# Another list order for the first 1278 operations of a fused attention and feed-forward kernel

## The chip, the cores and the metric

The kernel runs on one core of a Trainium2 chip. The metric is the device time of one execution in microseconds (us). Five engines take part, each with its own in-order queue: TensorE (PE in the profile, its weight loads PEld), VectorE (DVE), ScalarE (ACT), GpSimd (POOL) and SyncE (SP). SP only issues transfers here; sixteen DMA engines carry them out.

## The reference

Two blocks follow each other, all in float32. The first is a lightning attention over 4 batches, 8 heads, 768 positions and a head width of 64; the second a feed-forward block with a leaky ReLU.

```python
for b in range(nb):                                  # blocks of 64 positions
    intra = einsum('bhic,bhjc->bhij', qb, kb) * Dmask
    intra = einsum('bhij,bhjd->bhid', intra, vb)
    inter = einsum('bhid,bhde->bhie', qb * lam_pow, kv_state)
    out[:, :, sl] = intra + inter
    kv_state = lam_block * kv_state + einsum('bhsd,bhse->bhde', kb * rev_pow, vb)
x = out.transpose(0, 2, 1, 3).reshape(3072, 512)
h = x @ w_in                                         # 512 -> 2048
return maximum(0.01 * h, h) @ w_out                  # 2048 -> 512
```

## The kernel before

The 3072 rows are cut into 24 chunks of 128 tokens (the code's `c`); four chunks make a group (`g`, six in all). For each chunk the kernel loads k, q and v (`load_kq` L464, `load_v` L524), transposes k and q on PE through PSUM (L546), copies them out (`kT`, `qT`; L527, on ACT or DVE), scales q by powers of the decay (`qsT`, L592), scales k (L585, on POOL or DVE), and then runs small 64 x 64 products, all recorded at line L410: the scores (`go`, into `psc`), the key-value products (`kv`, into two spare PSUM banks for the first four chunks), the chunk's own part of the output (`own`) and two halves of the part that comes from the state (`inter`, before and after a two-column read `seen_po`, L676). DVE masks the scores (L637) and adds to the states (L642, L644); POOL decays the states (L647). The attention output of a chunk is then split into three parts, `xh` (ACT, L692), `xl` (DVE, L700) and `xm` (DVE, L718).

A float32 product of the feed-forward block is three products of rounded parts: high, low and mixed. The weights `w_in` are cut into eight pieces (`wi` 0 to 7, 256 columns each). A piece is loaded in two halves of 512 KB into one of three `raw` buffers, turned from 64-bit to 32-bit floats by three ACT operations (L793, L795, L797) and two DVE operations (L799, L800) a half, and split into `wh` (L805, on ACT or DVE), `wm` and `wl` (L812, L814, on DVE). Function `up` (L850) multiplies the parts of a group by those of a piece: six blocks of four products for each pair of group and piece (for the very first pair, group 0 and piece 1, in two calls of half width, 256 columns). ACT applies the leaky ReLU (L877) and the result goes to DRAM (L880). When all is through, `down` (L916) reads it back, splits it and multiplies by the parts of `w_out`.

The order of all this is not written as loops. The functions only add operations to a list (`Plan.add`): engine or engines that may do it, a length, what it reads and writes. `Plan.emit` then makes the program. It first takes the entries of `ORDER` (L266), a list of pairs of an operation's number and its engine, in exactly that order; where an operation may run on two engines, the pair also says on which. What `ORDER` doesn't list is placed behind it by a greedy rule. Since every engine's queue is in order, `ORDER` sets the order within each queue, SP's included, which issues each transfer when its turn comes and its target is free. The PSUM banks and buffers that are not fixed are handed out in list order too. A negative entry is a filler: `(-n, "PE")` runs `busy(n, ...)` (L344 to L349), products of the identity with itself, n blocks of 64 columns wide, whose result nobody reads. A fixed filler of nine blocks (`busy(WARM, ...)`) opens the program.

The numbers used below: for chunk 0, loads of k, q, v are 3, 4, 5, the transposes 6 and 7, copies 8 and 9, scaled k 10, scaled q 11, scores 12, key-value products 13, masked scores 14, first state 15, own output 19, state part 20, `seen_po` 21, second state part 22. Chunk 1 has the same in 26 to 45, chunk 2 in 49 to 70, chunk 3 in 72 to 94. Operations 101 and 95 load the two halves of weight piece 1, 171 and 177 those of piece 0; 155 to 160 and 163 to 168 are the half-width blocks of the first `up`. Operation 163, the first such block on chunks 2 and 3, is used as a milestone.

Each filler and product is issued by one of these two lines (L349, L850):

```python
nc.tensor.matmul(wide[:, :k, :], lhsT=ident, rhs=_bc(ident[:, 0:C2], 1, k), start=True, stop=True, skip_group_check=True)
nc.tensor.matmul(dst, lhsT=w[z][:, kk * 2 * P + f * P:kk * 2 * P + (f + 1) * P], rhs=x[z][:, kk, toks], ...
```

Of the kernel before, what the change touches and what calls it, by code (L numbers as in the profile page):

```python
# [239 lines left out]
def kernel(  # L240
# [117 lines left out]
    plan = Plan(kinds, also, {"k@2": early[0], "v@2": early[0], "k@3": early[1], "v@3": early[1], "q@3": early[2]})  # L358
    plan.fill, plan.idle, plan.warm, plan.order = busy, None if ORDER else busy, 1.3 + 0.22 * WARM, ORDER
    add = plan.add  # L360
# [680 lines left out]
```

## Time and profile before

| | |
|---|---|
| time, three runs | 610.72 us median (610.02 to 610.86) |
| the profiled execution | 610.24 us, of which the span on the core is 608.5 us |
| mean granted PE clock | 0.997 |
| DVE, ACT, POOL busy over the span | 48%, 35%, 12% |
| DVE busy from 30 to 75 us | 40.55 of 45.00 us |
| DVE busy from 75 to 90 us | 6.37 of 15.00 us |

The profile's page gives the span, the busy time of each engine, and a chain: the work that ended last, followed backwards. Its timeline lists instructions in order with the idle time before them and what ended it, in brackets. A table by stretches gives, for each stretch of time, the busy time and number of instructions of each engine, the granted PE clock, the share of the DMA engines and the rate moved. Ends of PE instructions are modelled, so that consecutive ones overlap by some tenths of a microsecond; distances between starts are the safer measure.

### The profile page before, as it was taken

The numbers are of one execution on the slowest core, as the hardware profiler recorded it, in microseconds if no ns is written. First come the engines' busy times: TensorE is split into PE (matmuls) and PEld (weight loads), VectorE is DVE, ScalarE is ACT, GpSimd is POOL, SyncE is SP. The second block draws the span as 40 slices with busy tenths as digits, with TensorE's granted clock in tenths as the row PEclk, the third lists the DMA queues.
The fourth block names the chain that finished last, engine by engine and source line by source line (L and its number), as shares of the span: only waits on it lengthen the run. The fifth ranks groups of instructions, "written<-read, shape, count | busy, mean of one in ns | idle before, by whom it ended". The sixth has DMA issues, their size and how long they took to land.

```text
span 608.5 us, 12711 instructions
## 1 busy us (share of the span) xinstructions
PE 598.8 (98%) x5368; PEld 493.6 (81%) x5368; DVE 291.6 (48%) x405; ACT 210.0 (35%) x326; POOL 74.6 (12%) x86
## 2 busy tenths in 40 slices
PE   7899999999999999999999999999999999999997
PEld 5688888888888888888788888888888888888886
DVE  6898936243164333343366864344353443534530
ACT  4667752221433423443434422222222313214111
POOL 3332312204041132122000000000000000000000
PEclk9899999999999999999999999999999999999999
DMA  9999866676798878876297852524434343433201
GB/s 210 215 262 273 215 195 166 155 166 183 175 279 229 226 197 216 231 205 205 86 360 282 311 163 79 174 69 140 137 104 138 104 137 117 127 104 122 87 1 69
DMA packets 147753, 105.18 MB, mean 173 GB/s; under 512 B 123632, under 2 KB 124400, under 8 KB 147696
## 3 DMA queue, kind: packets, MB, share of 16 engines
q1 hardware_dynamic: 147408, 104.29, 58.9%
q8 instruction: 42, 0.69, 0.5%
q14 instruction: 15, 0.12, 0.1%
q10 hardware_dynamic: 288, 0.07, 0.0%
HBM read 68.69 MB, written 35.65 MB: 171 GB/s over the span
## 4 chain that ended last, share of the span: by engine, by line
PE 95%; DMA 2%; SPq 1%; DVE 1%; issue 0%; ACT 0%; DVEq 0%
PE b L850 33%; PE b L916 16%; PE psc L916 11%; PE po L916 11%; PE pt L850 10%; PE pt L916 5%; PE po L410 4%; PE psc L410 3%; DMA gs<-in_v_dram 1%; SPq L466 1%; DMA att<-in_v_dram 1%; PE po L546 0%; DVE w L800 0%; DVE xm L718 0%; PE b L546 0%
## 5 line engine op out<-in xcount | busy, mean ns | idle before, releaser
L898 DVE SCALAR_TENSOR_TENSOR xl<-att,xh 128x1024 fp32r<-128x1024 f32 x48 | 58.7, 1222 | 126.4 <-ACT xh L897 126.4
L897 ACT ACTIVATE xh<-att 128x1024 fp32r<-128x1024 f32 x48 | 50.7, 1061 | 147.6 <-PE pt L916 69.9
L850 PE MATMUL b<-xl,wl 128*128 128x512 f32 (+1 forms) x300 | 78.2, 387 | 0.0
L850 PE MATMUL b<-xh,wh 128*128 128x512 f32 (+1 forms) x300 | 77.3, 388 | 0.0
L850 PE MATMUL b<-xm,wm 128*128 128x512 f32 (+1 forms) x300 | 77.2, 386 | 0.0
L877 ACT ACTIVATE gs<-b 128x512 f32<-128x512 f32 x73 | 42.3, 596 | 88.2 <-PE b L850 57.8
L850 PEld LDWEIGHTS b<-xh,wh 128*128 128x128 f32 x300 | 54.8, 188 | 11.4
L850 PEld LDWEIGHTS b<-xl,wl 128*128 128x128 f32 x300 | 54.9, 188 | 11.2
L850 PEld LDWEIGHTS b<-xm,wm 128*128 128x128 f32 x300 | 54.9, 188 | 11.1
L900 DVE SCALAR_TENSOR_TENSOR xm<-xl,xh 128x1024 fp32r<-128x1024 f32 x48 | 58.8, 1226 | 4.8
L916 PE MATMUL b<-wh,xh 128*128 128x512 f32 x144 | 56.0, 389 | 0.0
L916 PE MATMUL b<-wl,xl 128*128 128x512 f32 x144 | 56.0, 389 | 0.0
L916 PE MATMUL b<-wm,xm 128*128 128x512 f32 x144 | 56.0, 389 | 0.0
L647 POOL TENSOR_TENSOR att<-att 128x256 f32<-128x256 f32 x40 | 28.7, 718 | 125.4 <-DVE att L644 105.2
L916 PE MATMUL psc<-wm,xm 128*128 128x512 f32 (+1 forms) x100 | 38.2, 387 | 0.0
L916 PE MATMUL po<-wm,xm 128*128 128x512 f32 (+1 forms) x100 | 37.9, 384 | 0.0
L916 PE MATMUL psc<-wh,xh 128*128 128x512 f32 x96 | 37.3, 389 | 0.0
L916 PE MATMUL psc<-wl,xl 128*128 128x512 f32 x96 | 37.3, 389 | 0.0
L916 PE MATMUL po<-wh,xh 128*128 128x512 f32 x96 | 37.3, 389 | 0.0
L916 PE MATMUL po<-wl,xl 128*128 128x512 f32 x96 | 37.3, 389 | 0.0
L410 PEld LDWEIGHTS po<-att 64*64 64x64 f32 x1408 | 26.5, 134 | 10.3 <-issue 7.0
L410 PE MATMUL po<-att 64*64 64x64 f32 x1408 | 32.2, 222 | 1.9 <-DVE att L676 1.3
(105 smaller groups left out, 858.8 us busy)
## 6 DMA issues: line engine op xcount, KB each, us to landing
att<-g SPq DMA_DIRECT2D x48, 512.0 KB, 3.5
g<-gs SPq DMA_DIRECT2D x47, 512.0 KB, 3.5
raw<-in_moe_w_in_dram SPq DMA_DIRECT2D x16, 512.0 KB, 5.6
raw<-in_moe_w_out_dram SPq DMA_DIRECT2D x16, 512.0 KB, 4.6
out_dram<-gs SPq DMA_DIRECT2D x23, 256.0 KB, 2.1
att<-in_k_dram SPq DMA_DIRECT2D x44, 128.0 KB, 4.2
att<-in_v_dram SPq DMA_DIRECT2D x22, 256.0 KB, 4.4
wo<-w SPq DMA_DIRECT2D x8, 512.0 KB, 5.9
```

The costliest lines, as they stand in the source:

```text
L410: nc.tensor.matmul(dst[HALF[cols]], lhsT=lhsT[HALF[rows]], rhs=rhs[HALF[rows]], start=start, stop=True, skip_group_check=True)
L466: nc.sync.dma_start(out=dst[:, z * HP:(z + 1) * HP, :], in_=y[z::2].rearrange("h p d -> p h d"))
L647: add("POOL", 0.62, lambda new=new, j=j: nc.gpsimd.tensor_tensor(state[(j + 1) % 4], new, _bc(lam_c, 2, D), op=ALU.mult), [f"st{j % 4}", " ...
L850: nc.tensor.matmul(dst, lhsT=w[z][:, kk * 2 * P + f * P:kk * 2 * P + (f + 1) * P], rhs=x[z][:, kk, toks], start=start and kk == 0, stop=kk ...
L877: add("ACT", ns, lambda b=b, r=r: nc.scalar.activation(out=r(), in_=b(), func=AF.Prelu, bias=0.0, scale=1.0, alpha=0.01), [kb], [kg], rank ...
L897: add("ACT", 1.05, lambda: nc.scalar.activation(out=h, in_=graw[j], func=AF.Copy, bias=0.0, scale=NEAR), reads, wr("h"))
L898: add("DVE", 1.215, lambda: nc.vector.scalar_tensor_tensor(l, graw[j], 1.0, h.bitcast(F32), op0=ALU.mult, op1=ALU.subtract), reads + [f"rh ...
L900: add("DVE", 1.215, lambda: nc.vector.scalar_tensor_tensor(m, l.bitcast(F32), -S, h.bitcast(F32), op0=ALU.mult, op1=ALU.add), [f"rh{j}", f ...
L916: nc.tensor.matmul(to[:, cols], lhsT=ring[j][z][:, f * T + tb * P:f * T + (tb + 1) * P], rhs=W[pp][z][:, f * d_model:(f + 1) * d_model][:, ...
```

## The change

Only `ORDER` is replaced. It lists 1278 operations in place of 1276 (1290 and 1291, two PE blocks of `up`, are new in it) and eight fillers in place of two: of 5, 4, 10, 4, 4, 5, 4 and 5 blocks, where there were 10 and 9. The work that is computed is the same.

Twelve operations change engine. From ACT to DVE go 9, 31, 32 (the copies of `qT` of chunk 0 and of `kT` and `qT` of chunk 1), 21 (`seen_po` of chunk 0), 141, 686 and 783 (later `seen_po`). From DVE to ACT go 272, 601, 922 (`seen_po`) and 324 and 399 (`wh` of pieces 4 and 6).

In SP's queue, the loads after the first half of weight piece 1 stood in the order v of chunk 1, k of chunk 2, second half of piece 1, q and v of chunk 2, q and k of chunk 3, first half of piece 0, q of chunk 4, second half of piece 0, v of chunk 3. They now stand: k and q of chunk 2, v of chunk 1, second half of piece 1, q of chunk 3, v of chunk 2, q of chunk 4, k and v of chunk 3, the two halves of piece 0.

On PE, the two transposes of chunk 0 change places, the scores of a chunk come earlier against the products of the chunk before it, and four half-width blocks of `up` (155 to 158) stand together ahead of the key-value products of chunk 3, where only one (155) did. The transpose of chunk 4's k (113) and its key-value products (128), which stood ahead of 163, come behind it; the scores of chunk 4 (129), which stood between 165 and 166, come behind 166. From some 300 blocks on the orders fall together again: the last 236 planned operations of PE, 105 of DVE, 79 of ACT and 81 transfers are the same.

```diff
-    ORDER = [(4, "DMA"), (0, "DVE"), (2, "DVE"), (3, "DMA"), (1, "DVE"), (26, "DMA"), (5, "DMA"), (-10, "PE"), (6, "PE"),
-      (27, "DMA"), (101, "DMA"), (7, "PE"), (29, "PE"), (8, "DVE"), (28, "DMA"), (9, "ACT"), (12, "PE"), (49, "DMA"), (31, "ACT"),
-      (10, "POOL"), (11, "DVE"), (13, "PE"), (30, "PE"), (33, "POOL"), (14, "DVE"), (15, "DVE"), (32, "ACT"), (19, "PE"), (20, "PE"),
-      (21, "ACT"), (35, "PE"), (34, "DVE"), (102, "ACT"), (95, "DMA"), (50, "DMA"), (51, "DMA"), (73, "DMA"), (16, "POOL"),
-      (72, "DMA"), (17, "DVE"), (105, "DVE"), (103, "ACT"), (22, "PE"), (37, "DVE"), (36, "PE"), (18, "POOL"), (23, "ACT"),
...
-      (82, "PE"), (64, "POOL"), (-9, "PE"), (81, "PE"),
...
+    ORDER = [(4, "DMA"), (3, "DMA"), (26, "DMA"), (0, "DVE"), (-5, "PE"), (7, "PE"), (1, "DVE"), (5, "DMA"), (2, "DVE"), (27, "DMA"),
+      (9, "DVE"), (-4, "PE"), (6, "PE"), (10, "POOL"), (101, "DMA"), (49, "DMA"), (8, "DVE"), (-10, "PE"), (12, "PE"), (11, "DVE"),
+      (14, "DVE"), (29, "PE"), (33, "POOL"), (13, "PE"), (31, "DVE"), (50, "DMA"), (15, "DVE"), (103, "ACT"), (19, "PE"), (102, "ACT"),
+      (30, "PE"), (28, "DMA"), (20, "PE"), (32, "DVE"), (95, "DMA"), (21, "DVE"), (34, "DVE"), (16, "POOL"), (73, "DMA"), (-4, "PE"),
+      (35, "PE"), (37, "DVE"), (22, "PE"), (52, "PE"), (-4, "PE"), (53, "PE"), (105, "DVE"), (104, "ACT"), (17, "DVE"), (23, "ACT"),
+      (106, "DVE"), (-5, "PE"), (36, "PE"), (54, "ACT"), (24, "DVE"), (55, "ACT"), (97, "ACT"), (58, "PE"), (18, "POOL"), (25, "DVE"),
+      (42, "PE"), (96, "ACT"), (38, "DVE"), (43, "PE"), (57, "DVE"), (98, "ACT"), (39, "POOL"), (44, "DVE"), (60, "DVE"), (45, "PE"),
+      (40, "DVE"), (46, "ACT"), (51, "DMA"), (111, "DMA"), (72, "DMA"), (56, "POOL"), (99, "DVE"), (100, "DVE"), (47, "DVE"), (76, "PE"),
+      (-4, "PE"), (59, "PE"), (41, "POOL"), (-5, "PE"), (114, "PE"), (74, "DMA"), (107, "ACT"), (48, "DVE"), (171, "DMA"), (65, "PE"),
+      (177, "DMA"), (61, "DVE"), (66, "PE"), (78, "ACT"), (116, "ACT"), (67, "ACT"), (108, "DVE"), (75, "PE"), (77, "ACT"), (68, "PE"),
+      (69, "ACT"), (109, "DVE"), (155, "PE"), (82, "PE"), (156, "PE"), (157, "PE"), (158, "PE"),
...
```

2 lines of the change are left out of this document (1 added, 1 removed).

## The prediction

> **What bounds the kernel now.** I read the page's head first, then who PE waits for, then a table by stretches, then PE's timeline.
>
> ```profile
> span 608.5 us, 12711 instructions
> PE 598.8 (98%) x5368; PEld 493.6 (81%) x5368; DVE 291.6 (48%) x405; ACT 210.0 (35%) x326; POOL 74.6 (12%) x86
> ...
> PE 95%; DMA 2%; SPq 1%; DVE 1%; issue 0%; ACT 0%; DVEq 0%
> ...
> PE po L410 <- DVE att L676: 1.3, 1, 1.3
> PE b L410 <- DMA att<-in_v_dram: 1.1, 1, 1.1
> PE b L410 <- DMA gs<-in_v_dram: 0.9, 1, 0.9
> ```
>
> PE is busy 598.8 of 608.5 us and makes up 95% of the chain, so only some 10 us are not PE work. The three longest of PE's waits but the one at the start are for a two-column read on DVE and for two loads of v (the last number of a row is the longest single wait). The table says where they lie:
>
> ```profile
> 11.50:19.70 8.20, 4.46 (x141) 3.64 (x140) 7.29 (x13) 6.61 (x11) 3.41 (x4) 0.98 0.93 212
> 19.70:23.10 3.40, 3.40 (x84) 2.64 (x84) 2.75 (x5) 1.38 (x3) 1.33 (x1) 0.55 1.01 244
> 23.10:28.50 5.40, 4.55 (x132) 3.46 (x127) 4.29 (x7) 4.17 (x8) 1.84 (x3) 1.00 0.98 239
> 28.50:34.30 5.80, 5.66 (x115) 4.79 (x107) 5.38 (x10) 3.30 (x7) 1.36 (x2) 1.00 1.04 297
> 34.30:75.00 40.70, 40.70 (x683) 34.30 (x676) 36.67 (x55) 28.98 (x53) 12.27 (x12) 1.00 0.91 246
> 75.00:304.70 229.70, 229.70 (x2759) 189.31 (x2758) 87.34 (x174) 82.14 (x147) 50.98 (x56) 1.00 0.72 194
> 304.70:608.50 303.80, 300.49 (x1329) 248.87 (x1327) 141.78 (x124) 79.98 (x98) 0.00 (x0) 1.00 0.42 141
> ```
>
> (Columns: stretch and length; busy time of PE, PEld, DVE, ACT, POOL; granted PE clock; DMA share; GB/s.) From 11.5 to 19.7 PE stands idle 3.74 of 8.20 us, then works 3.4 us at a clock of 0.55, then idles 0.85 more. From 34.3 to 304.7 it is never idle. DVE is nearly full too: 36.67 of 40.70 us up to 75 us; later it has room. So what can be won lies before 34 us, and what may take it away is DVE between 30 and 75 us.
>
> ```profile
> 12.60 0.69 PE L410 MATMUL b<-att 64*64 64x64 f32 x32 [1.09 <-DMA att<-in_v_dram]
> ...
> 20.01 1.13 PE L410 MATMUL b<-gs 64*64 64x64 f32 x32
> ...
> 25.53 1.29 PE L349 MATMUL b<-att 128*128 128x512 f32 x4
> 27.67 0.69 PE L410 MATMUL b<-gs 64*64 64x64 f32 x32 [0.85 <-DMA gs<-in_v_dram]
> ...
> 28.62 0.78 PE L410 MATMUL po<-att 64*64 64x64 f32 x16
> ...
> 30.31 0.73 PE L850 MATMUL b<-xl,wl 128*128 128x256 f32 x4
> ...
> 32.12 0.66 PE L546 MATMUL po<-att 128*128 128x128 f32 x4
> ...
> 34.32 0.74 PE L850 MATMUL b<-xh,wh 128*128 128x256 f32 x4
> ...
> 294.88 1.19 PE L850 MATMUL b<-xh,wh 128*128 128x512 f32 x4
> 296.00 0.46 PE L410 MATMUL po<-att 64*64 64x64 f32 x16
> ...
> 303.82 1.07 PE L850 MATMUL b<-xl,wl 128*128 128x512 f32 x4
> 304.73 1.07 PE L850 MATMUL b<-xm,wm 128*128 128x512 f32 x4
> ```
>
> The row at 34.32 is operation 163, my milestone. The row at 304.73 is where PE's order becomes the same in both kernels; all behind it (303.8 us with the tail) I cost at nothing: it is PE back to back, ACT and DVE have the same order there too, and its cover is DVE at 47%. The same 32 small products take 0.69 us at 12.60 and 1.13 us at 20.01: the half clock. Over 3.4 us at 0.55 it costs about 3.4 x 0.45 = 1.5 us.
>
> **The change, part by part.** *Loads.* When do they land in the new queue order?
>
> ```profile
> 11.27 0.66 ACT L793 ACTIVATE w<-raw 128x512 f32<-128x512 f32 x1 [0.30 <-DMA raw<-in_moe_w_in_dram]
> 15.81 0.78 ACT L795 ACTIVATE low<-raw 128x512 uint16<-128x512 uint32 x1 [1.30 <-DMA raw<-in_moe_w_in_dram]
> ...
> 20.66 6.88 DMA gs<-in_v_dram
> ```
>
> ACT waits for both halves of weight piece 1, so these rows date their landings: 11.27 and 15.81. Between them came v of chunk 1, k of chunk 2 and the half itself, 1.0 MB in 4.54 us: 1.14 us per 256 KB. In the new order v of chunk 1 lands behind k and q of chunk 2: 11.27 + 3 x 1.14 = 14.7 instead of 12.6. The second half of piece 1: 15.81 + 1.14 = 17.0. v of chunk 2, behind q of chunk 3: 19.2. v of chunk 3, the load that PE waited for until 27.67 (the last row: issued 20.66, 6.88 us to landing): 17.0 + 5 x 1.14 = 22.7, five us earlier. So one of the two waits for v goes, the other is moved. The loads of later pieces stand one 512 KB transfer (2.3 us) further back; they have ACT's slack before them, and I cost that at nothing; without it DVE waits as long.
>
> *DVE, up to chunk 3's state.* What is late next is DVE's list, so I add it up.
>
> ```profile
> 5.54 1.57 DVE L386 TENSOR_TENSOR_SCAN att<-att 128x64 f32<-128x64 f32 x8
> 7.03 0.67 DVE L527 COPY att<-pt 128x512 f32<-128x512 f32 x1
> ...
> 28.48 0.42 DVE L644 TENSOR_TENSOR att<-att,b 128x256 f32<-128x256 f32 x1 [0.54 <-PE b L410]
> ...
> L637 DVE TENSOR_TENSOR att<-psc,att 128x512 f32<-128x512 f32 x4 | 2.7, 680 | 0.5 <-PE psc L410 0.5
> L799 DVE TENSOR_SCALAR w<-w 128x512 int32<-128x512 int32 x4 | 2.3, 577 | 1.1 <-ACT w L793 1.0
> L800 DVE CUSTOM_DVE_ANT_0 w<-w,low 128x1024 uint16<-128x1024 uint16 x2 | 2.2, 1119 | 0.1
> L644 DVE TENSOR_TENSOR att<-att,b 128x256 f32<-128x256 f32 x5 | 2.1, 415 | 1.4 <-PE b L410 1.4
> L814 DVE SCALAR_TENSOR_TENSOR wl<-wm,wh 128x1024 fp32r<-128x1024 f32 x1 | 2.1, 2065 | 0.0
> L700 DVE TENSOR_TENSOR xl<-po,xh 128x512 fp32r<-128x512 f32 x3 | 2.0, 680 | 0.0
> L592 DVE TENSOR_TENSOR att<-b,att 128x512 f32<-128x512 f32 (+1 forms) x3 | 1.8, 599 | 0.8 <-ACT att L527 0.8
> L812 DVE SCALAR_TENSOR_TENSOR wm<-wh,w 128x1024 fp32r<-128x1024 f32 x1 | 1.2, 1218 | 0.0
> L718 DVE SCALAR_TENSOR_TENSOR xm<-xl,xh 128x512 fp32r<-128x512 f32 x1 | 0.7, 693 | 0.0
> ```
>
> The decay tables end at 7.1 in either order. Then, new on DVE, the copies of `qT` and `kT` of chunk 0 (0.67 each): 8.5. Scores on PE 0.7, masked scores 0.68: 9.9. Copy of `kT` of chunk 1 and first state: 11.0. PE reaches the transposes of chunk 1's q behind one transpose and two groups of small products (some 0.5 each), at 11.3; copy: 12.0; `seen_po` and scaled q: 12.8; masked scores 0.68 and a shift (L799): 14.0. Three moved copies and `seen_po` are 2.2 us more on DVE, but it idled 0.47 to 0.8 us at these places before, as the idle times of the groups (0.5 and 0.8) show.
>
> From 14.0 to the state of chunk 3 (the row at 28.48) the new list has 22 operations: six L642 or L644 (2.5 us), two L637 (1.4), three L700 (2.0), two L718 (1.4), two L592 of full size (1.4), two L799 (1.2), two L800 (2.2), L812 (1.2), L814 (2.1) and a `seen_po` (0.15): 15.5. Ends are modelled some 0.06 over the next start, 1.4 for 22. With 0.8 of short waits (chunk 1's second state part, the half that lands at 17.0 behind three ACT conversions, chunk 3's scores) DVE is through at 28.9. Before: 28.48 + 0.42 = 28.9. So DVE wins nothing here, though it has one L718 more behind it.
>
> *PE up to the milestone.* Before, PE still had 5.7 us from 28.62 to 34.32. In the new order three of the half-width blocks (156 to 158) are done by then, between 25 and 28 us where PE ran a filler (25.53) and waited 0.85; 113 and 128 are put behind 163. What remains: the two state parts and the q transposes, 30.31 - 28.62 = 1.7 less 0.3 in which the first waited for the state, 1.4; and two blocks at (32.12 - 30.31)/3 = 0.6, a wait included, so 0.55 each: 1.1. Milestone at 28.9 + 1.4 + 1.1 = 31.4, **2.9 us earlier**.
>
> *Fillers.* 41 blocks instead of 19. The row at 25.53 is nine blocks in 1.29 us, so 22 more are up to 3.2 us. They lie ahead of operations that by the dates above wait anyway (the copies at 8.5 and 12.0, v at 14.7 and 19.2); bound: 0 to 3.2, taken 0, since the DVE dates contain no filler. If those waits are shorter than I think, a filler makes them as long as itself.
>
> *Behind the milestone.* Before: 304.73 - 34.32 = 270.4 us. 113 and 128 come in: 34.32 - 32.12 less two blocks, 2.2 - 1.2 = **+1.0**. The new order goes 20 times from wide blocks to small products instead of 23; a block next to small ones lasts 296.00 - 294.88 = 1.12, one among its like 304.73 - 303.82 = 0.91, so about 0.1 for each of three passages: **-0.3**. And DVE: from 28.9 to chunk 4's `xl` (146) its new list sums to 17.8 us by the same durations, 46.7. PE wants it for 188 after 6 half blocks (3.3), 7 full ones (6.5), 4 transposes (2.0), 7 small groups (3.0): 14.8 us behind 31.4, at 46.2. A stall of **+0.5**; bounds 0 and 2.9 (all of the lead). `wl` of piece 0, wanted six us behind the milestone, comes within 0.3 of it.
>
> Sum: -2.9 + 1.0 - 0.3 + 0.5 = -1.7 us against the profiled execution's 610.24: 608.5. The median of the runs stands 0.48 above that execution, so **609.0 us**.
>
> *The clock.* The row at 19.70 shows the half clock behind a stretch in which PE idled 46% but never longer than 1.3 us. [...]
>
> **Rivals.** *DVE keeps the lead for itself* (0.12). DVE reaches 28.9 no earlier than before, and its list to 75 us is shorter by little: two `wh` copies (some 0.7 each) go to ACT. If it sets the pace, PE's lead shrinks to the extra L718 (0.7): 610.0. For it: 36.67 of 40.70. Against: 4 us of its idle time there.
>
> *The half clock stays* (0.10). PE still has short waits from 12 to 28 us. If the clock halves once, 1.5 us: 610.5. Against: eight fillers stand in them.
>
> *Slower: DVE's in-order waits stop PE* (0.28). From 31 to 75 us DVE idled 4.0 us in the old order without harm, since PE was behind it. With PE 2.9 us earlier each wait of DVE for a PE result is paid by PE in full. Above 1.7 + 1.2 = 2.9 us more of such waits the kernel is slower than before; doubled (4.0) they give 613.0, less the slack that the later blocks have, some 612.
>
> **How the numbers follow.** Forecast 0.50. 0.2% is 1.2 us, about what a measurement of this kernel tells from no change: faster means below 609.5, slower above 611.9. The first two rivals are no change (0.22). The range reaches down to all of the lead without stall and with two us of passages and short waits less, -3.7: 607.0; up to the slower rival at 612.2. The forecast's own range is 607.0 to 609.9.
>
> **What would show it.** Right: PE's first wide group of four half blocks at 24 to 27 us, no wait for v of chunk 3, a clock of 1.00 at 20 us, operation 163 near 31.4, the block at 304.73 near 303.0. Wrong: PE waits for DVE (L700, L814) between 35 and 60 us; a row of clock below 1; the second half of piece 1 landing much behind 17.0, which moves chunk 1's split and all behind it one for one.

## The result and the profile after

| | before | after |
|---|---|---|
| time, six runs each | 610.79 us median (610.02 to 611.12) | 608.21 us median (607.59 to 609.12) |
| the profiled execution; its span | 610.24 us; 608.5 us | 608.22 us; 606.4 us |

The ratio is 0.9961, with a 95% interval of 0.9949 to 0.9974: 0.4% faster. A later batch (the tenth experiment) gave 607.24 us for the same kernel against 610.04 us, ratio 0.9949 (0.9936 to 0.9961). So times of different batches differ by up to 1 us, and below I compare ratios, or positions inside a profiled execution.

The head of the page of the kernel after, its chain, and the rows of PE's waits:

```profile
span 606.4 us, 12716 instructions
PE 598.9 (99%) x5378; PEld 494.1 (81%) x5378; DVE 291.5 (48%) x405; ACT 214.0 (35%) x326; POOL 74.4 (12%) x86
...
PE 93%; SPq 3%; DMA 2%; issue 0%; POOL 0%; DVE 0%; ACT 0%; DVEq 0%; POOLq 0%
...
PE b L349 <- POOL att L352: 1.4, 1, 1.4
PE pt L410 <- DMA gs<-in_v_dram: 1.1, 1, 1.1
```

PE is busy as long as before (598.9 against 598.8 us); the span lost 2.1 us of its idle time. The two busy times are alike by chance: 22 more blocks of filler count as busy now, and the stretch at half clock is gone. Of the three long waits of before one load of v is left, now that of chunk 2. The stretches, with the columns of the prediction's table:

```profile
11.50:19.70 8.20, 7.13 (x188) 4.85 (x186) 7.03 (x16) 5.84 (x10) 3.27 (x4) 1.00 0.96 211
19.70:23.10 3.40, 2.67 (x87) 2.19 (x87) 3.33 (x6) 2.18 (x4) 1.21 (x1) 1.00 0.88 212
23.10:28.50 5.40, 5.12 (x140) 4.45 (x136) 4.36 (x8) 3.40 (x7) 2.56 (x3) 1.00 1.00 275
...
34.30:75.00 40.70, 40.70 (x696) 34.16 (x697) 33.17 (x51) 28.73 (x52) 10.12 (x11) 1.00 0.97 265
75.00:304.70 229.70, 229.40 (x2759) 189.40 (x2758) 91.80 (x176) 86.71 (x151) 52.18 (x56) 1.00 0.75 204
```

PE stands idle 1.07 of 8.20 us in the first stretch where it stood 3.74, partly because fillers count as busy. The clock stays at 1.00 where it was 0.55. From 34.3 to 75 us PE is again never idle.

PE's timeline after, at the places that the prediction dated:

```profile
20.43 0.24 PE L410 MATMUL pt<-gs 64*64 64x64 f32 x1 [1.05 <-DMA gs<-in_v_dram]
...
21.70 0.60 PE L546 MATMUL b<-att 128*128 128x128 f32 x4
...
24.42 0.74 PE L850 MATMUL pt<-xh,wh 128*128 128x256 f32 x4 [0.28 <-ACT att L527]
...
25.71 0.74 PE L850 MATMUL pt<-xl,wl 128*128 128x256 f32 x4
26.29 0.64 PE L850 MATMUL pt<-xh,wh 128*128 128x256 f32 x4
26.77 0.64 PE L850 MATMUL pt<-xl,wl 128*128 128x256 f32 x4
27.34 0.69 PE L410 MATMUL b<-gs 64*64 64x64 f32 x32
...
31.05 0.63 PE L850 MATMUL b<-xh,wh 128*128 128x256 f32 x4
...
46.28 0.60 PE L546 MATMUL po<-att 128*128 128x128 f32 x4
...
129.24 0.46 PE L410 MATMUL psc<-att 64*64 64x64 f32 x16 [0.30 <-DVE att L518]
...
302.69 1.07 PE L850 MATMUL pt<-xm,wm 128*128 128x512 f32 x4
```

The milestone (operation 163) is the row at 31.05, 3.27 us earlier than before. Three of the half-width blocks that before stood behind chunk 3's products are the rows at 25.71, 26.29 and 26.77. The row at 302.69 is the block that before stood at 304.73 (the name of its bank is another): the gain has shrunk to 2.04 us, and stays so to the end. The row at 24.42 opens the first wide group; from it to the milestone it takes 6.63 us here, and 6.62 to 7.00 in every later run of the new head but the sixth. So what dates the milestone is when that group can begin.

### The profile page after: what moved, and what is told of

Read it like the earlier page. It is cut to its first block, busy times and chain, and to the rows that moved or that the text cites. A ratio compares the mean times of both kernels' runs of the same rounds, so it can differ in the third digit from the quotient of the medians.

```text
span 606.4 us, 12716 instructions
## 1 busy us (share of the span) xinstructions
PE 598.9 (99%) x5378; PEld 494.1 (81%) x5378; DVE 291.5 (48%) x405; ACT 214.0 (35%) x326; POOL 74.4 (12%) x86
## 4 chain that ended last, share of the span: by engine, by line
PE 93%; SPq 3%; DMA 2%; issue 0%; POOL 0%; DVE 0%; ACT 0%; DVEq 0%; POOLq 0%
PE b L850 31%; PE b L916 16%; PE pt L850 11%; PE psc L916 11%; PE po L916 11%; PE pt L916 5%; PE po L410 4%; PE psc L410 3%; SPq L466 1%; DMA gs<-in_v_dram 1%; SPq L509 1%; DMA raw<-in_k_dram 1%; SPq L524 0%; PE po L546 0%; PE b L546 0%
## 5 line engine op out<-in xcount | busy, mean ns | idle before, releaser
L850 PE MATMUL b<-xl,wl 128*128 128x512 f32 (+1 forms) x288 | 75.9, 389 | 0.0
L850 PE MATMUL b<-xh,wh 128*128 128x512 f32 (+1 forms) x288 | 75.6, 390 | 0.0
L850 PE MATMUL b<-xm,wm 128*128 128x512 f32 (+1 forms) x288 | 75.4, 390 | 0.0
L850 PEld LDWEIGHTS b<-xl,wl 128*128 128x128 f32 x288 | 53.3, 188 | 11.0
L850 PEld LDWEIGHTS b<-xm,wm 128*128 128x128 f32 x288 | 53.1, 188 | 11.0
L850 PEld LDWEIGHTS b<-xh,wh 128*128 128x128 f32 x288 | 53.1, 188 | 11.0
L799 DVE TENSOR_SCALAR w<-w 128x512 int32<-128x512 int32 x32 | 17.4, 552 | 36.3 <-ACT w L793 35.9
```

Source lines behind the costliest of these rows:

```text
L799: add("DVE", 0.42, lambda: nc.vector.tensor_scalar(d, d, 3, None, op0=ALU.logical_shift_left), [], [key], lock=True)
```

## The experiments

Only `ORDER` is edited, so the work computed is the same but for fillers. A diff shows the entries that change at that place. "Milestone" is the start of operation 163, "block" that of the block that before stood at 304.73.

**Head alone and tail alone.** The first takes the new list up to 163 and the old one behind it (operations 180 and 174 exchanged, so that buffers go round as before); the second does the reverse.

```diff
 (160, "PE"), (163, "PE"),
-(93, "DVE"), (87, "POOL"), (113, "PE"), (164, "PE"), (215, "DMA"), (174, "ACT"), (182, "DVE"), (209, "DMA"),
+(180, "ACT"), (182, "DVE"), (176, "DVE"), (93, "DVE"), (215, "DMA"), (113, "PE"), (183, "ACT"), (209, "DMA"),
...
```

> The new order up to operation 163 (the milestone), the old order behind it. Theory (all of the gain lies ahead of the milestone, from work done in former waits and a clock that does not halve): milestone at 31.0 us as in the new kernel, 3.3 us earlier than before; operations 113 and 128, now behind it, give 1.0 back; DVE may stop PE once for 0.5: 608 to 609 us, ratio to before 0.995 to 0.997. Rival (the old tail needs DVE results at the old times, so DVE takes the lead back): PE waits for DVE between 31 and 60 us, 610 to 611 us, ratio 0.999 to 1.000.

> The old order up to operation 163, the new order behind it. Theory: milestone at 34.3 us as before, and nothing is won behind it but three passages from wide to small products (0.3 us): 610.2 to 610.9 us, ratio 0.999 to 1.000. Rival (the order behind the milestone carries part of the gain): 608.5 to 609.7 us, ratio 0.996 to 0.998.

The first gave 612.11 us, ratio 1.0019 (1.0005 to 1.0033): the head alone loses. The second gave 610.56 us, ratio 0.9995 (0.9986 to 1.0004): the tail alone does nothing. So the two parts do not add up; the head's lead is only kept by the tail that goes with it. Rows of PE in the first kernel (its stops and the milestone), and the row of DVE that stands ahead of the split of chunk 3:

```profile
20.97 0.33 PE L410 MATMUL b<-gs 64*64 64x64 f32 x2 [0.97 <-issue]
...
32.74 0.63 PE L850 MATMUL b<-xh,wh 128*128 128x256 f32 x4
35.17 0.66 PE L546 MATMUL po<-att 128*128 128x128 f32 x4 [1.79 <-DVE xl L700]
36.61 0.58 PE L410 MATMUL psc<-att 64*64 64x64 f32 x24 [0.79 <-DVE att L585]
...
65.62 0.85 PE L850 MATMUL b<-xl,wl 128*128 128x512 f32 x3 [1.56 <-issue]
```
```profile
33.22 1.29 DVE L800 CUSTOM_DVE_ANT_0 w<-w,low 128x1024 uint16<-128x1024 uint16 x2 [1.03 <-ACT low L797]
```

This execution, at 614.36 us, is the second slowest of its twelve. The milestone leads by 1.6 us and not by the 3.3 that were expected: PE stopped for 1 us at 20 us with no partner ("issue"), and the clock fell to half from 21.6 to 25.0 us, which it did not do in the kernel after. PE then stands 2.6 us for DVE: the split of chunk 3 (`xl`, which reads the bank that PE's next transposes need) and the scaled k of chunk 4 are where the old list has them, which was early enough for a PE that came later. The diff shows it for `xl` (93): it stands behind 182 and 176, two operations of L800, and DVE waited 1.03 us for ACT ahead of these. A further 1.6 us has no partner; both stops are taken up below.

**Fillers.** The third leaves the five late fillers out of the new kernel; the fourth puts 28 blocks of filler into the idle places of the old one.

```diff
-(-4, "PE"), (35, "PE"),
+(35, "PE"),
...
```

> The new order without its five later fillers (4, 4, 5, 4 and 5 blocks); the three at the start stay. Theory (the fillers stand in waits and only hold the clock): PE idles some 4 of the 8.2 us from 11.5 to 19.7, the clock halves once for 3.4 us, and since part of that lies in waits the time is 0.5 to 1.5 us above the new kernel: 608.7 to 609.7 us. Rival 1 (short gaps do not halve the clock): clock 1.00 throughout, within 0.3 us of the new kernel. Rival 2 (the fillers hold up real work): 0.3 to 1 us below the new kernel.

It gave 607.82 us, ratio 0.9951 (0.9939 to 0.9963), within the interval of the kernel after. In its profiled execution the clock did halve, and the milestone hardly moved:

```profile
11.50:19.70 8.20, 5.64 (x214) 4.71 (x212) 7.77 (x17) 5.60 (x11) 3.38 (x4) 1.00 1.10 238
19.70:23.10 3.40, 2.70 (x53) 2.28 (x54) 3.33 (x5) 2.06 (x4) 1.54 (x1) 0.60 0.81 188
```
```profile
20.40 1.09 PE L546 MATMUL b<-att 128*128 128x128 f32 x4 [0.79 <-DMA att<-in_q_dram]
...
24.65 0.74 PE L850 MATMUL pt<-xh,wh 128*128 128x256 f32 x4 [0.28 <-ACT att L527]
...
31.28 0.64 PE L850 MATMUL b<-xh,wh 128*128 128x256 f32 x4
```

The milestone alone misleads. From the transposes of chunk 4's q (114; 20.40, after: 21.70) to the wide group (24.65, after: 24.42) PE took 4.25 us here and 2.72 in the kernel after, with the same single wait of 0.28 between: the half clock cost 1.53 us. The milestone is only 0.2 us late because these transposes began 1.3 us earlier in this execution, in which PE's wait for v of chunk 2 ended at 18.92 instead of 20.43.

Each execution's mean clock is on record, and one stretch of 3.41 us at half clock, as the trace of the kernel before has it from 19.36 to 22.77 us, lowers it by 3.41 x 0.5 / 608 = 0.003. In the new order with its fillers (after and tenth) none of 12 executions shows it. Without the late fillers two of six do in the third (608.37 and 608.87 us; the others 607.20 to 608.44) and three of six in the ninth (607.28 to 607.58; the others 606.65 to 606.90). In the old order it is common and costs 0.1 to 0.8 us: 51 of 63 executions of the kernel before show it, and by batch their medians lie that much above those of the other 12 (609.94 to 610.15 us). So the late fillers do hold the clock; by these few executions that gain is about as large as what they cost, and in the medians neither shows. Among executions at full clock the kernel after is still some 2 us faster (608.21 and 607.24 us): most of the gain is not the clock.

```diff
-(36, "PE"),
+(-9, "PE"), (36, "PE"),
...
-(45, "PE"),
+(-10, "PE"), (45, "PE"),
...
```

> The old order with four fillers more, ahead of the four PE operations that waited longest between 11.5 and 19 us: 9 blocks ahead of the key-value products of chunk 1, 4 ahead of its own output, 10 ahead of its second state part, 5 ahead of the scores of chunk 2. Theory: the clock stays at 1.00 from 19.7 to 23.1 us, and of the 1.5 us that the half clock cost some 0.5 to 1.5 show in the end, the rest being taken by DVE's list: 609.3 to 610.3 us. Rival (the half clock has another cause than the gaps): a stretch at half clock as before, 610.5 to 611.5 us.

It gave 612.32 us, ratio 1.0030 (1.0018 to 1.0042). The fillers did what they could: the clock is 1.00 where it was 0.55, and stayed up in six of the twelve executions. The milestone came only 0.16 us earlier, and a stall that was not there before costs more:

```profile
19.70:23.10 3.40, 3.40 (x107) 2.66 (x105) 3.24 (x6) 1.74 (x5) 1.88 (x2) 1.00 1.02 255
```
```profile
34.16 0.74 PE L850 MATMUL b<-xh,wh 128*128 128x256 f32 x4
...
60.58 0.44 PE L546 MATMUL b<-att 128*128 128x128 f32 x2
63.23 0.44 PE L546 MATMUL b<-att 128*128 128x128 f32 x2 [2.22 <-issue]
```

**A stall without a partner.** PE stops here in the middle of a group of four transposes of the same tile, and the profile finds nothing that it waits for. The page has a queue named "instruction" (packets, MB, share of 16 engines), the same in the kernels before and after:

```profile
q8 instruction: 42, 0.69, 0.5%
```

One packet is 0.69 MB / 42 = 16 KB. What a packet holds, and whether PE waits for one, the profile does not show; that PE stops at a fixed count of its instructions was my theory, and the next run tests it by adding some. The fifth kernel is the old one with its first filler cut into eight. Each filler call of up to eight blocks stands in the trace as two products, so six calls more are 12 products with their weight loads, 24 instructions, and no work (the fourth kernel's fillers were 12 products more, too).

```diff
-(-10, "PE"), (6, "PE"),
+(-1, "PE"), (-1, "PE"), (-1, "PE"), (-1, "PE"), (-1, "PE"), (-1, "PE"), (-1, "PE"), (-3, "PE"), (6, "PE"),
```

> The old order; only its first filler of 10 blocks is issued as eight products of 1, 1, 1, 1, 1, 1, 1 and 3 blocks instead of two of 8 and 2, in the same idle time at the start. That is 24 more PE instructions, as in the old order with four late fillers, where PE stood 2.2 us at 61 us while a 16 KB block of its instructions was on the way. Theory (PE runs out of instructions at a fixed count of them, and 24 more move that point into a stretch of small products that uses them up faster than they are fetched): an idle of 1.5 to 2.3 us that the profile puts down to issue near 60 to 64 us, 612.0 to 613.2 us. Rival (the late fillers themselves cost it): 610.5 to 611.0 us and no such idle.

It gave 612.57 us, ratio 1.0026 (1.0014 to 1.0039), and the stall at the same place of the order. The profile now names a load of v that PE's transposes do not need:

```profile
61.01 0.44 PE L546 MATMUL b<-att 128*128 128x128 f32 x2
63.43 0.44 PE L546 MATMUL b<-att 128*128 128x128 f32 x2 [1.99 <-DMA att<-in_v_dram]
```

Set beside the start times of that queue's eighth packet, and counted over PE's instructions in the traces:

```
kernel                      packet starts   PE instructions     longest distance of
                            (took), us      begun by then       two products after it
before                      60.34 (0.96)    2194                0.32 us
fourth (old, more filler)   60.80 (0.96)    2241                2.49 us, at instruction 2241
fifth (old, +24)            61.18 (0.97)    2241                2.26 us, at instruction 2241
first (new head, old tail)  63.43 (0.97)    2235                2.04 us, at instruction 2240
eleventh (first, -20)       63.07 (0.96)    2158                0.32 us
after                       55.68 (1.24)    2203                0.34 us
```

In the three kernels in which PE had begun 2235 to 2241 instructions when the packet started, it stops at 2240 or 2241 and goes on 1.47, 1.28 and 1.22 us after the packet has ended (fourth, fifth, first). In the three in which it had begun 2158 to 2203, no two products after it stand more than 0.34 us apart.

In three versions of the new head PE also stopped near 20 us: in the first (from 19.78 to 20.97), the seventh (19.91 to 21.33) and the eighth (20.20 to 21.22). The waits of the seventh and of the eighth name no partner either:

```profile
PE b L410 <- issue: 1.2, 1, 1.2
```
```profile
PE pt L410 <- issue: 0.8, 1, 0.8
```

So 24 instructions more bring the stop near 61 us, in the fifth run with almost no work in them. What PE waits for at any of these stops no trace shows.

**Which part of the new head makes the lead.** The sixth puts the half-width blocks 156 to 158 (with 159 behind them) back behind 123; the seventh issues the second half of weight piece 1 (95) behind k of chunk 3 (73); the eighth puts the four copies 9, 21, 31 and 32 back on ACT.

```diff
-(155, "PE"), (82, "PE"), (156, "PE"), (157, "PE"), (158, "PE"), (172, "ACT"),
+(155, "PE"), (82, "PE"), (172, "ACT"),
...
-(123, "PE"),
+(123, "PE"), (156, "PE"), (157, "PE"), (158, "PE"), (159, "PE"),
```

> The new order with the three half-width blocks 156 to 158 put back behind the q transpose of chunk 5 (123), where the old order has them. Theory (the gain is these blocks done while PE would wait): PE waits 1.6 us more between 24 and 29 us, milestone 1.6 us later, 609.5 to 610.1 us. Rival (DVE and the loads set the dates behind the milestone anyway): less than 0.5 us, 608.0 to 608.7 us.

It gave 608.63 us, ratio 0.9968 (0.9956 to 0.9980): the median is inside the rival's range. The profiled execution, at 609.8 us the slowest of its five, shows what was expected of it, with the clock halved besides:

```profile
19.70:23.10 3.40, 3.04 (x38) 2.31 (x38) 2.83 (x5) 1.27 (x2) 1.36 (x1) 0.57 0.81 209
23.10:28.50 5.40, 4.07 (x133) 3.24 (x133) 3.33 (x5) 4.22 (x8) 1.61 (x3) 0.95 1.02 265
```
```profile
25.59 0.74 PE L850 MATMUL pt<-xh,wh 128*128 128x256 f32 x4 [0.28 <-ACT att L527]
...
28.10 0.69 PE L410 MATMUL b<-gs 64*64 64x64 f32 x30 [1.05 <-DVE att L644]
...
33.39 0.65 PE L850 MATMUL b<-xh,wh 128*128 128x256 f32 x4
```

PE idles 1.33 of 5.40 us where the blocks had been, and the milestone is 2.3 us later than after. Half of that is not the blocks: the first block is already 1.17 us late (25.59 against 24.42), behind the half clock. From it to the milestone it takes 7.80 us instead of 6.63, at full clock: the blocks are worth 1.17 us there, where 1.6 was expected. What they are worth in the median is not settled: 0.4 us by the two medians of different batches, with intervals that overlap.

```diff
-(95, "DMA"), (21, "DVE"), (34, "DVE"), (16, "POOL"), (73, "DMA"),
+(21, "DVE"), (34, "DVE"), (16, "POOL"), (73, "DMA"), (95, "DMA"),
```

> The new order with the load of the second half of weight piece 1 one place further back, behind q of chunk 3: it lands some 1.1 us later (18.4 instead of 17.3), q of chunk 3 some 2 us earlier. Theory (this half stands in ACT ahead of the split of chunk 1, and all that follows moves with it one for one): milestone 0.8 to 1.1 us later, 609.0 to 609.3 us. Rival (v of chunk 2, which lands at 20.3, sets the dates): within 0.4 us of the new kernel, 607.8 to 608.6 us.

It gave 607.95 us, ratio 0.9951 (0.9939 to 0.9963). The half landed at 18.1 instead of 17.3 us and the milestone at 31.57, half a microsecond later than after; the time did not follow. The time shows no one-for-one shift. The milestone cannot decide it: the stop of 1.2 us near 20 us lies ahead of it, and the kernel after has none there.

```diff
-(9, "DVE"),
+(9, "ACT"),
...
-(31, "DVE"),
+(31, "ACT"),
...
-(32, "DVE"), (95, "DMA"), (21, "DVE"),
+(32, "ACT"), (95, "DMA"), (21, "ACT"),
```

> The new order with the three copies and the two-column read of chunks 0 and 1 back on ACT. Theory of the prediction (DVE's list, added up from the first copies, sets the dates): 2.2 us less on DVE give a milestone 0.5 to 1.5 us earlier, 606.7 to 607.7 us. Rival (the loads of v of chunk 1 at 15.1, of the weight half at 17.3 and of v of chunk 2 at 20.3 set them): scores of chunk 1 earlier, but the milestone within 0.4 us, 607.8 to 608.6 us.

It gave 607.42 us, ratio 0.9945 (0.9933 to 0.9957), milestone at 31.46. Three copies of 0.67 us and a `seen_po` less on DVE did not bring it forward, but this milestone too has a stop near 20 us ahead of it (0.8 us). A better sign that DVE's early list does not set the milestone is the tenth run below, which reached it at 30.40 with the copies on DVE, and the ninth, which reached it at 30.44 without them.

**Do two small things add up?** The third and the eighth looked a little faster than the kernel after. The ninth has both edits, and the tenth, beside it on the same chip, is the kernel after itself.

> The new order with both the four copies (9, 31, 32, 21) back on ACT and the five late fillers left out. If each of the two is worth by itself what its ratio showed (0.9945 and 0.9951 against the 0.9961 of the new order), they add up to about 607.0 us (606.7 to 607.3), with the row of operation 163 at 31.0 to 31.5. Rival: the two only look better because they ran beside other runs of the kernel before; then this one and the unchanged new order, run beside it, come out within 0.6 us of each other. With the idle places of PE unfilled the clock is also free to halve once; by the run without late fillers that costs no more than 0.3 us.

> The new order unchanged, as the measure for the kernel beside it: 608.2 us (607.6 to 608.8), ratio 0.996, operation 163 at 31.0 to 31.5, no idle place of PE over 0.4 us between 34 and 75 us.

The ninth gave 607.09 us, ratio 0.9948 (0.9934 to 0.9962), the tenth 607.24 us, ratio 0.9949 (0.9936 to 0.9961). They are the same; the rival was right, and no version found here beats the kernel after. The milestone's row of the ninth, then of the tenth:

```profile
30.44 0.64 PE L850 MATMUL b<-xh,wh 128*128 128x256 f32 x4
```
```profile
30.40 0.64 PE L850 MATMUL b<-xh,wh 128*128 128x256 f32 x4
```

The tenth is the same program as after, and its milestone is 0.65 us earlier. That is the scatter against which the sixth to eighth have to be read: the seventh's and eighth's do not stand out of it, and of the sixth's 33.39 it is the distance from the wide group that does.

**The first again with fewer instructions.** The eleventh is the first without its five late fillers, 20 instructions of PE less; each of the five edits is as in the third's diff.

> The first experiment (new order up to operation 163, old order behind it) without its five late fillers, which are 20 instructions of PE (10 products with their weight loads). Theory: of the loss of that run, the idle place of 1.6 us near 65 us with no waiting partner is PE having run out of fetched instructions; with the count of instructions back at that of the kernel before it goes, and the time is 610.0 to 610.8, so that the old tail takes back all of the lead through DVE and nothing more. Rival: the idle place belongs to the order of the work, stays at 1.5 us or more within 60 to 68 us, and the time stays at 611.6 to 612.4.

It gave 611.62 us, ratio 1.0024 (1.0012 to 1.0037), the rival's time. But the rival's reason is gone: PE has no idle place near 65 us. Its waits, two stretches, and its rows:

```profile
PE pt L410 <- DMA gs<-in_v_dram: 1.9, 1, 1.9
PE po L546 <- DVE xl L700: 1.8, 1, 1.8
...
PE psc L410 <- DVE att L585: 0.8, 1, 0.8
```
```profile
34.30:36.80 2.50, 1.72 (x37) 1.36 (x37) 1.83 (x2) 1.52 (x4) 0.00 (x0) 0.76 1.02 350
36.80:40.20 3.40, 3.40 (x38) 2.88 (x37) 1.23 (x1) 2.92 (x6) 0.00 (x0) 0.68 1.15 319
```
```profile
31.83 0.64 PE L850 MATMUL b<-xh,wh 128*128 128x256 f32 x4
...
307.72 1.07 PE L850 MATMUL b<-xm,wm 128*128 128x512 f32 x4
```

From milestone to block it takes 307.72 - 31.83 = 275.9 us, where the kernel after takes 302.69 - 31.05 = 271.6. The 4.3 us are PE's two waits for DVE (1.80 + 0.78, the same as in the first) and a half clock behind them (0.24 x 2.50 + 0.32 x 3.40 = 1.7). So the stall went with the 20 instructions, as my theory had it, though no trace shows that PE had run out of them; my time did not hold: in this execution, which at 613.28 us lies above its median, the half clock took the stall's place, at a spot where no later wait absorbs it. The recorded clocks say how often: it fell in 11 of the 12 executions (610.91 to 614.22 us), and the one at full clock took 610.11 us, within the theory's range. In the first, with the fillers, it fell in five of 12 (median 613.86 us; the seven others 611.43).

## Why the prediction was right, step by step

*Loads.* The half of weight piece 1 was dated 17.0. ACT began on it at 17.34. PE's wait for v of chunk 2 ended at 20.43, where I had the landing at 19.2, and chunk 3's first product with v (27.34) has no wait at all. The row of ACT and those of DVE's dates, after:

```profile
17.34 0.80 ACT L795 ACTIVATE low<-raw 128x512 uint16<-128x512 uint32 x1 [1.86 <-DMA raw<-in_moe_w_in_dram]
```
```profile
13.32 0.43 DVE L799 TENSOR_SCALAR w<-w 128x512 int32<-128x512 int32 x1
...
25.85 0.69 DVE L637 TENSOR_TENSOR att<-psc,att 128x512 f32<-128x512 f32 x1 [0.74 <-PE psc L410]
...
28.16 0.42 DVE L644 TENSOR_TENSOR att<-att,b 128x256 f32<-128x256 f32 x1 [0.30 <-PE b L410]
...
45.16 0.68 DVE L700 TENSOR_TENSOR xl<-po,xh 128x512 fp32r<-128x512 f32 x1
```

*DVE's list.* The masked scores of chunk 1 and the shift were to be through at 14.0 and chunk 3's state at 28.9. They are through at 13.32 + 0.43 = 13.75 and 28.16 + 0.42 = 28.58. The dates were good to 0.3 us, but for the second that is luck: DVE waited for PE's scores ahead of 25.85 (0.74 us) and for PE's products ahead of 28.16 (0.30 us), so from there on PE's dates set DVE's and not the list.

*Milestone.* 31.4 was forecast, 31.05 measured (30.40 in the tenth run): -2.9 against -3.3. The first wide group stands where the prediction put it (24.42 to 27.4). The three half-width blocks done early carry part of it: 1.17 us by the sixth run's profiled execution, in which moving them back lengthened the way from the wide group to the milestone by that much. No run takes 113 and 128 (1.0 us in the prediction) or the loads apart from them.

*Fillers at nothing.* The net is confirmed by the medians of the third and ninth runs. It is a balance, as the clocks of their executions show, and not a cost of nothing.

*Behind the milestone.* The sum of this part was right and its terms were not, which is luck. I had +1.0 for 113 and 128, -0.3 for passages and +0.5 for a stall on DVE at operation 188: +1.2. Measured: 271.64 - 270.41 = +1.23. The stall at 188 is the step that failed: its row at 46.28 has no wait. My list was too long. I summed it to 17.8 us from DVE's date of 28.9 on; DVE did it in 14.99 us of work, and `xl` was through at 45.16 + 0.68 = 45.84, 0.4 us ahead of PE, although DVE waited 1.59 us for PE on the way. One duration that I used was 2.07 us for `wl`; there it took 1.23. The passages I can read from the tail alone: in the second run the milestone is at 34.62 and the block at 304.62, so 270.00 us, 0.4 less than before. That leaves 1.6 us where I had 1.0 for the two operations moved in; 0.3 of it is the one short wait at 129.24, which I had not foreseen, and the rest I have no row for. What lies behind the block costs 606.4 - 302.69 = 303.7 us against 303.8: nothing, as said.

*Sum.* -1.7 us was forecast for the span; it is 606.4 - 608.5 = -2.1, and -2.6 between the medians.

*The rivals.* "DVE keeps the lead for itself" was wrong as to the new order: DVE is busy 3.5 us less in that stretch, not "shorter by little", and 4.5 us more behind 75 us, where it has room (91.80 against 87.34). "The half clock stays" didn't come true: the clock fell in none of the 12 executions of the new order. Its price of 1.5 us was right where PE waits for nothing behind it, as ahead of the wide group in the third run (1.53) and in the eleventh (1.7). In whole times a half clock cost the new order without late fillers 0.7 to 1.4 us by the medians of the ninth and third, and the kernel before 0.1 to 0.8. "DVE's in-order waits stop PE" didn't come true of the change, but the first and eleventh runs show that very mechanism with the old tail: 2.6 us of waits, and the kernel slower than before. The chance that I gave it was a chance that the tail would not fit, and it fits. None of the rivals had the stops without a partner, which held the same head for 1.0, 1.2 and 0.8 us in the first, seventh and eighth runs.

## What to carry to other kernels

A lead won at the start of a long in-order program is worth only what the lists of the other engines behind that point let through: move their operations forward with it, and test head and tail apart, since they need not add up. Price a lower clock, a filler or a shorter list by the waits that follow it, not by its own length; and read such a price between two rows that have no wait between them, not from one date that other things move too. And where the profile names nothing for a stall, or something that the instruction does not read, test whether it moves with the number of instructions ahead of it: 24 added instructions that do almost no work cost 1.7 us here.

## What the runs showed of the hardware that was not expected

PE stopped for 2.0 to 2.5 us in the middle of a group, at its instruction 2240 or 2241 in three different kernels, beside a 16 KB packet of the instruction queue that took 0.96 or 0.97 us and started when PE was there already or within five instructions of it; with 20 instructions less, or in the kernel before, it did not (longest distance of two products 0.32 us). It stopped for 1.0 to 1.4 us near 20 us in three kernels of the new head. Ahead of the longer stop PE issues small products fast (54 products of 64 x 64 in 0.98 us, fourth and fifth runs). What it waited for at these stops stays open.

The half clock of the kernel before is one stretch of 3.41 us (19.36 to 22.77, granted clock 0.50). In these runs neither the idle share of a stretch nor the longest wait says where the clock falls: the sixth run, with PE busy 6.76 of 8.20 us from 11.5 to 19.7, lost it behind a wait of 1.4 us (0.57 from 19.7 to 23.1), and the ninth, busy 6.18 of 8.20, kept it behind one of 2.2 (1.00). What sets it no run here was made to show, and it stays open.
